# Copying u from PSUM instead of moving it by DMA, two output stores per block, and a new hand-written order

## The chip, the cores and the metric

The kernel runs on one core of a Trainium2 chip. The metric is the device time of one execution in microseconds (us), the median of several runs. The core has five engines that each work through their own instruction stream in order: PE (TensorE, matmuls), DVE (VectorE), ACT (ScalarE), POOL (GpSimd) and SP (SyncE, which here only issues DMA transfers). ACT issues some DMA transfers too.

## What is computed

The inputs r, k, v, w, a, b have the shape (4, 8, 768, 40): batch, heads, time steps, head width. For each of the 32 pairs of batch and head a 40x40 state is carried over the 768 steps:

```python
for t in range(S):
    y[:, :, t] = np.einsum('bhd,bhde->bhe', rt, state)
    Sa = np.einsum('bhde,bhe->bhd', state, at)
    state_decay = state * wt[:, :, None, :] - np.einsum('bhd,bhe->bhde', Sa, bt)
    state = state_decay + np.einsum('bhd,bhe->bhde', vt, kt)
```

The result, laid out as x of shape (4, 768, 320), goes through a gated convolution over time and two matrix products:

```python
h = np.maximum(x @ w_in, 0.0)            # w_in: 320 x 1024
conv_out = sum(conv_w[k] * hp[:, k:k + S, :] for k in range(3))   # hp is h, padded by one step on each side
gate = 1.0 / (1.0 + np.exp(-conv_out))
out = (h * gate) @ w_out                 # w_out: 1024 x 320
```

## The kernel before

**Tiling.** The 768 time steps are cut into 24 chunks of 32 (`C`, `NSTEP`); two chunks make a pair (index `j`, 12 of them) and also a window of 64 steps for the second part (`W`, 12 windows). Inside a chunk the recurrence is replaced by matrix products with a small triangular inverse.

**Per pair:** `load_wakb` brings in w, a, k, b; `decays` makes running products of w (`suf`, `pre`, two scans each on DVE); `decayed` makes the scaled a, k and b (`ah`, `kt`); `scores` multiplies them (`ps`) into `at`; `solve_in` writes a part of `at` through DRAM into `bb`; `solve` runs 31 dependent multiply-add pairs (`st`, `xx`, lines L566 and L572), for even pairs on DVE and for odd ones on POOL; the inverse `tt` comes back through DRAM.

**Per chunk n, the chain** (`chain`): `pp` = state times a, plus scores times v (PE, L598 and L608); `psb` = -pp (ACT, L615); `pu` = tt times psb (PE, L624), which is u in PSUM; then u goes into the tile `vu`. That tile has 128 partitions (four quadrants of 32) and a free index y of 0 or 1 in front of the heads; v has been loaded into two of the four quadrants for each y, and u fills the other two. After that `pn` = vu times kb (PE, L647), the new state = old state + pn (DVE, L659; in the first chunk a copy, L657) and its decay (POOL, L662), with which the next chunk starts. There are two `vu` tiles and two state tiles, used in turn.

**How u gets beside v before:** ACT copies all of `pu` into an SBUF tile `u` (L631), then ACT issues three transfers from `u` into `vu` (L635): quadrant 0 and quadrant 3 into y=1, and quadrants 1 and 2 together into y=0. `pn` and `pv` wait for all three.

**Outputs per chunk:** `vturn` turns vu (`pv`, L671, copied by ACT into `v`, L688); `pairs` makes `pm` and `ms`; `from_state` and `outputs` add up `py`; `finish` turns it (`pq`, L774), scales it (`xf`, DVE, L779) and splits it into `xh` (ACT) and `xl` (POOL).

**Per window:** `moe_in` makes four pieces `ph` (16 matmuls each, L814), the relu `hb`, the convolution `cc` (ACT L835, DVE L843), the sigmoid (ACT L848) and the gate product `g` (DVE L853); `moe_out` makes two blocks `po` (16 matmul instructions each, L861). A block covers two batches of 64 steps: 128 rows of 320 numbers. ACT copies it into the only buffer `ob` (L876) and SP stores it: in window 0 by two transfers of 63 rows (L882), in the other windows by one transfer whose DRAM side has the shape 2 x 64 x 320 (L886). At the end `moe_end` makes the last time step from `pe` (L861) through the same buffer, as `oe` (L907, L908).

**Weights** come as float64 words and are made into float32 by DVE, eight instructions a piece (L267 to L285), 23 pieces, all in the first third of the run.

**What sets the order.** Nothing is scheduled by a planner at run time: the table `ORDER` lists tokens such as `ch5` (the chain of chunk 5) or `mi3.2` (piece 2 of window 3), and each token lets that piece of work emit its instructions up to its next `yield`. So the table decides how the pieces are mixed in every engine's stream. A chain has nine such parts for n > 0; the fifth is the copy to `u`, the sixth the three transfers.

Of the kernel before, what the change touches and what calls it, by code (L numbers as in the profile page):

```python
# [17 lines left out]
C = 32  # L18
# [5 lines left out]
    tt=2, psb=1, u=1, sd=1, r64=1, vu64=1, ms=1, ysb=1, xf=1, xh=2, xl=2, xp=1, hb=2, cc=2, o=1,  # L24
# [9 lines left out]
we0 we1 ld0*2 we0 ld0 lv0*2 we1 we0 de0 we2 ld0*2 de0*2 dd0 we1 ld1 lv1*2 we2 we3 lr0*2 dd0*2 we2  # L34
we1*2 dd0*4 we2*2 ld1 dd0 we0*2 de1 ha0 de1*2 we4 ha0*2 fs0*2 dd0*2 we3 rt0 ha1 rt0*2 ha1*2 ld1 we3
dd1 we3*2 we4 we5 ld1*2 ld2 sc0 dd1*2 we4*3 we6 sc0*2 dd1 sc1 lr1*2 ch0 sc1*2 dd1 we5 dd1 we5 ch0
we5*2 dd1*2 de2 we7 de2*2 ha2 si0*2 ha2*2 we7 dd1*2 we6 we7*3 we8 so0 we6 ld2 we6*2 we9 ld2*3 so0
sc2*3 sc3*3 so0 dd2 si1*2 we9 so0 we9*3 we10 so0 ld3 so0*3 we8 so0*2 so1*2 we10 we8 dd2*2 we10*3
dd2*4 we11 we8*2 dd2 so1 we12 ch0 dd2*2 ch0*2 so1 ld3 we11 ld3 so1 sc4 we12 we11 we13 ch0*2 we12*3
sc4*2 vt0 we11*2 we14 sc5 lv2*2 vt0*2 ch0*2 sc5*2 ro0 pa0 so1 si2*2 pa0*2 ch1*2 we13*2 st1 ch1*2  # L40
st1*2 ou0 ch1 we14*2 ch1 so1 ha3*3 we15 we16 ou0*2 fs1*2 ro0*2 fi0*2 so1 fi0*3 vt1 we15*2 ch1 vt1*2
pa1 we17 pa1*2 so1*2 ch1 ou1 we16*2 ha4 ch1*2 ou1*2 fi1 ha4*2 rt1 ch2 rt1*2 fi1 ch2 we17*2 fi1 de3
ch2 fi1*2 st2*3 pk0*2 mi0.3*2 de3*2 we18 we19 ld3*2 ch2 so2 lv3*2 dd3 ch2*2 mi0.2*2 ld4 mi0.3
we19*2 mi0.2 fs2*2 mi0.3 mi0.2 we20 we18*2 mi0.3 lr2*2 mi0.2 vt2 we21 vt2*2 dd3*2 ch2 dd3*2 lv4*2
ch2 dd3*2 ch2*2 we20*2 pa2 we22 ld4 dd3 we21*2 st3 dd3*2 st3*2 ch3*2 pa2*2 we22*2 ch3 ou2 ld4 ch3
ou2*2 fi2 ch3 ha5 ch3 fi2 fs3*2 mi0.3 sc6 ha5*2 fi2 sc6*2 sc7 mi0.3 fi2*2 sc7*2 mi0.3*2 mi0.0 si3*2
mi0.1 mi0.2 mi0.1 vt3 ch3 so2 vt3*2 mi0.2 pa3 mi0.1 pa3*2 ch3 ou3 lv5*2 mi0.2*2 rt2 ch3*2 ou3*2
mi0.1*2 so2 fi3 lr3*2 mi0.0 rt2*2 st4*3 ch4*2 fi3 so2 fi3 mi0.0 fi3*2 pk1*2 de4 ha6 mi0.0 ch4 de4*2
dd4 ha6*2 mi0.0 ld4*2 ld5 so2 fs4*2 so2*3 mi0.1 so2*2 so3 dd4*2 mi0.1 so3 mi0.1*2 mi1.2 mi1.3 dd4*5
mi0.0 so3 dd4*2 mi0.0 mi1.3*2 ch4 mi0.0*2 mi1.0 ch4 so3 ch4 ld5 mi1.3*3 ld5 mi1.0*2 sc8 mi1.0*2  # L50
# [87 lines left out]
def tile_decay_delta_attention_then_conv_gate_moe(  # L138
# [45 lines left out]
    def quad(i):  # L184
        return slice(C * i, C * i + C)
# [829 lines left out]
```

## Time and profile before

| | before |
|---|---|
| median of 3 runs | 742.21 us (738.25 to 743.95) |
| the profiled execution, its own time | 741.73 us |
| its span, first to last instruction | 740.0 us |
| PE busy | 576.2 us (78%), 14265 matmuls |
| DVE busy | 439.7 us (59%), 1043 instructions |
| ACT busy (issuing transfers not counted) | 238.9 us (32%), 529 instructions |
| POOL busy | 228.9 us (31%), 466 instructions |
| mean granted TensorE clock | 0.835 of full speed |

Busy shares are averages over stages with different limits, so the profile is read by stage: when an engine is idle, the row of its next instruction says what ended last before it. The span is the part in which instructions ran; the execution's own time is 1.7 us longer.

### The profile page before, as it was taken

How to read it: one execution, taken by the hardware profiler on the slowest of the kernel's cores; microseconds unless marked ns; L12 is line 12 of the kernel's file. 1: busy time of each engine (PE TensorE's matmuls, PEld its weight loads, DVE VectorE, ACT ScalarE, POOL GpSimd, SP SyncE). 2: the span in 40 equal slices, each digit the busy share in tenths (PEclk: the TensorE clock that was granted, in tenths of full speed). 3: DMA queues.
4: the chain of work that ended last, by engine and by line, in shares of the span. 5: the costliest groups of instructions: out<-in, count | busy, mean ns of one | idle time of the engine just before them, and what ended most of it. 6: DMA issues, size and time to landing. Idle time of an engine off the chain costs nothing.

```text
span 740.0 us, 31943 instructions
## 1 busy us (share of the span) xinstructions
PE 576.2 (78%) x14265; PEld 490.5 (66%) x14265; DVE 439.7 (59%) x1043; ACT 238.9 (32%) x529; POOL 228.9 (31%) x466
## 2 busy tenths in 40 slices
PE   3634076678488788988988969889887998789995
PEld 2523065567377668777777858788687786768882
DVE  8878945966963764454874524965715695422550
ACT  1210012314232423434333135135333344344551
POOL 5101582001285101374002345014820017711100
PEclk9755557958868997997996899979977999899998
DMA  8999477673475356465563464644655425121000
GB/s 147 168 134 147 99 127 132 136 131 62 73 127 94 59 117 103 64 118 93 101 127 66 81 124 71 126 107 86 117 100 78 105 47 98 28 51 40 19 26 20
DMA packets 285345, 69.40 MB, mean 94 GB/s; under 512 B 258496, under 2 KB 281048, under 8 KB 285208
## 3 DMA queue, kind: packets, MB, share of 16 engines
q1 hardware_dynamic: 249280, 59.36, 44.6%
q10 hardware_dynamic: 35928, 7.99, 6.0%
q8 instruction: 112, 1.84, 1.1%
q14 instruction: 25, 0.20, 0.1%
HBM read 38.63 MB, written 10.22 MB: 66 GB/s over the span
## 4 chain that ended last, share of the span: by engine, by line
PE 47%; DVE 17%; DMA 14%; issue 7%; POOL 6%; SPq 3%; ACT 2%; ACTq 2%; DVEq 0%; POOLq 0%
PE po L861 9%; PE ph L814 9%; DMA vu<-u 4%; PE ps L510 3%; PE pm L715 3%; DVE xx L572 3%; PE pv L671 3%; PE pn L647 3%; DVE st L566 3%; PE py L753 2%; PE pu L624 2%; POOL st L566 2%; POOL xx L572 2%; PE pt L698 2%; PE pp L608 2%
## 5 line engine op out<-in xcount | busy, mean ns | idle before, releaser
L861 PE MATMUL po<-wo,g 128*128 128x320 f32 x384 | 117.6, 449 | 1.3 <-ACT hb L828 1.3
L843 DVE SCALAR_TENSOR_TENSOR cc<-hb,cw,cc 128x256 f32<-128x256 f32 x192 | 90.0, 532 | 44.1 <-ACT cc L835 44.1
L566 POOL TENSOR_TENSOR st<-xx,bb 128x126 f32<-128x126 f32 (+22 forms) x186 | 73.3, 394 | 67.5 <-DMA bb<-bd 31.3
L861 PEld LDWEIGHTS po<-wo,g 128*128 128x128 f32 x384 | 70.9, 196 | 26.1 <-issue 2.0
L662 POOL TENSOR_TENSOR state<-state,a 104x640 f32<-104x640 f32 x23 | 33.6, 1460 | 157.9 <-DVE state L659 139.2
L572 POOL TENSOR_TENSOR xx<-xx,st 128x126 f32<-128x126 f32 (+22 forms) x186 | 74.8, 402 | 14.6
L789 POOL TENSOR_TENSOR xl<-xf,xh 120x384 fp32r<-120x384 f32 x24 | 25.5, 1062 | 169.4 <-ACT xh L787 165.0
L814 PE MATMUL ph<-xh,wih 120*128 120x256 f32 x288 | 62.5, 330 | 0.8 <-ACT ob L876 0.8
L510 PE MATMUL ps<-a,k 40*64 40x32 f32 x1536 | 37.8, 249 | 29.0 <-issue 15.7
L828 ACT ACTIVATE hb<-ph 128x512 f32<-128x512 f32 x48 | 28.5, 598 | 91.0 <-PE ph L814 78.5
L510 PEld LDWEIGHTS ps<-a,k 40*64 40x64 f32 x1536 | 34.2, 168 | 34.1 <-issue 26.0
L572 DVE TENSOR_TENSOR xx<-xx,st 128x126 f32<-128x126 f32 (+22 forms) x186 | 52.7, 283 | 6.4
L566 DVE TENSOR_TENSOR st<-xx,bb 128x126 f32<-128x126 f32 (+22 forms) x186 | 50.7, 272 | 7.0 <-DMA bb<-bd 1.2
L814 PEld LDWEIGHTS ph<-xh,wih 120*128 120x128 f32 x288 | 46.8, 214 | 5.2 <-issue 1.6
L624 PE MATMUL pu<-psb,tt 32*32 32x40 f32 x1536 | 27.5, 230 | 26.8 <-DVE ah L460 17.5
L722 DVE TENSOR_TENSOR ms<-pm,tri 128x512 f32<-128x512 f32 x24 | 16.6, 690 | 48.7 <-PE pm L715 48.5
L853 DVE TENSOR_TENSOR g<-cc,hb 128x512 f32<-128x512 f32 x48 | 34.5, 728 | 18.3 <-ACT cc L848 9.1
L779 DVE TENSOR_TENSOR xf<-pq,pre 120x384 f32<-120x384 f32 x24 | 13.3, 554 | 52.6 <-PE pq L774 48.3
L624 PEld LDWEIGHTS pu<-psb,tt 32*32 32x32 f32 x1536 | 22.8, 132 | 32.1 <-issue 27.8
L835 ACT ACTIVATE cc<-hb,cw 128x256 f32<-128x256 f32 x96 | 42.6, 501 | 0.0
L814 PE MATMUL ph<-xl,wih 120*128 120x256 f32 x192 | 42.3, 304 | 0.1
L516 DVE TENSOR_TENSOR at<-ps,tris 128x512 f32<-128x512 f32 x24 | 16.6, 690 | 42.6 <-PE ps L510 42.6
(305 smaller groups left out, 1155.9 us busy)
## 6 DMA issues: line engine op xcount, KB each, us to landing
bb<-bd SPq DMA_DIRECT2D x24, 256.0 KB
w<-in_w_dram SPq DMA_DIRECT2D x24, 160.0 KB
a<-in_a_dram SPq DMA_DIRECT2D x24, 160.0 KB
k<-in_k_dram SPq DMA_DIRECT2D x24, 160.0 KB
vu<-in_v_dram SPq DMA_DIRECT2D x96, 40.0 KB
b<-in_b_dram SPq DMA_DIRECT2D x24, 160.0 KB
rin<-in_r_dram SPq DMA_DIRECT2D x24, 160.0 KB
k<-kt SPq DMA_DIRECT2D x24, 160.0 KB
```

The source lines that it names most:

```text
L510: nc.tensor.matmul(ps[half(z), x, y * 128 + hp * C : y * 128 + hp * C + C], k64[half(x, D), 2 * y + c, kp, z], a64[half(x, D), c, y, hp, z ...
L566: eng.tensor_tensor(t3, xx[:, 0:nj, i : i + 1].to_broadcast([128, nj, nt]), bb[:, i : i + 1, i + 1 :].to_broadcast([128, nj, nt]), ALU.mult,)
L572: eng.tensor_tensor(xx[:, 0:nj, i + 1 :], xx[:, 0:nj, i + 1 :], t3, ALU.add)
L624: nc.tensor.matmul(pu[bu(bi), 0, h * D : h * D + D], pd["tt"][quad(bi), c, 4 * x + hp], psb[quad(bi), x, hp], start=(h == 0), stop=True, s ...
L662: nc.gpsimd.tensor_tensor(new, new, al[..., 0:1].to_broadcast([SR, 2, 8, D]), ALU.mult)
L789: nc.gpsimd.tensor_tensor(wd["xl"][:, :, :, tw], xf, xh.bitcast(F32), ALU.subtract)
L814: nc.tensor.matmul(ph[:, j], l[:, fs], x, start=(j == 0 and i == 0), stop=(i == len(passes) - 1), skip_group_check=True,)
L828: nc.scalar.activation(out=hb[:, :, :, 2 : W + 2], in_=ph, func=AF.Relu)
L835: nc.scalar.activation(out=cc[:, j], in_=hb[:, j, :, 1 : W + 1], func=AF.Copy, scale=cw[:, 1, f : f + 1],)
L843: nc.vector.scalar_tensor_tensor(out=cc[:, j], in0=hb[:, j, :, x : W + x], scalar=cw[:, x, f : f + 1], in1=cc[:, j], op0=ALU.mult, op1=ALU ...
L853: nc.vector.tensor_tensor(g, cc, hb[:, :, :, 1 : W + 1], ALU.mult)
L861: nc.tensor.matmul(po[:rows, :DM], parts(f), wo[:, f, :], start=(f == 0), stop=(f == NF - 1))
```

## The change

Three things change.

1. The tile `u` and the three transfers go. Four copies read `pu` directly and write into `vu`, one for each quadrant of 32 partitions and 320 columns: ACT takes quadrants 1 and 2, DVE takes quadrants 0 and 3. Both reach their place without leaving their partitions, since only the free index y differs. The chain has one part less.
2. Every output block is stored by two transfers, one per batch (64 rows, in window 0 still 63), as it was before in window 0 alone.
3. The table `ORDER` is new throughout; of it the diff shows one line of each.

```diff
-    tt=2, psb=1, u=1, sd=1, r64=1, vu64=1, ms=1, ysb=1, xf=1, xh=2, xl=2, xp=1, hb=2, cc=2, o=1,
+    tt=2, psb=1, sd=1, r64=1, vu64=1, ms=1, ysb=1, xf=1, xh=2, xl=2, xp=1, hb=2, cc=2, o=1,
...
-pa1 we17 pa1*2 so1*2 ch1 ou1 we16*2 ha4 ch1*2 ou1*2 fi1 ha4*2 rt1 ch2 rt1*2 fi1 ch2 we17*2 fi1 de3
+vt1 we18 fs1*2 lv3*2 vt1*2 fi0*2 ch1 pa1 so1 rt1 pa1*2 ou1 lr2*2 rt1*2 ha3 ou1*2 ch1*2 fi1 ha3*2
...
-        uu = buf(wn, [128, H, D], "u", f"u{n}")
-        nc.scalar.copy(uu.rearrange("p h d -> p (h d)"), pu[:, 0, 0:HD])
-        yield
-
-        for rows, y in ((slice(0, C), 1), (slice(3 * C, 4 * C), 1), (slice(C, 3 * C), 0)):
-            nc.scalar.dma_start(vu[rows, y, :, 0:D], uu[rows])
+
+        for i, q in enumerate((1, 0, 2, 3)):
+            dst = vu[quad(q), int(q in (0, 3)), :, 0:D]
+            src = pu[quad(q), 0, 0:HD].rearrange("p (h d) -> p h d", d=D)
+            if i % 2:
+                nc.vector.tensor_copy(dst, src)
+            else:
+                nc.scalar.copy(dst, src)
         yield
...
-        if lo:
-            for x in range(BO):
-                nc.sync.dma_start(
-                    out[bo * BO + x, t0 - 1 + lo : t0 + W - 1, :], ob[x * W + lo : (x + 1) * W]
-                )
-        else:
-            nc.sync.dma_start(out[bs, t0 - 1 : t0 + W - 1, :], ob)
+        for x in range(BO):
+            nc.sync.dma_start(
+                out[bo * BO + x, t0 - 1 + lo : t0 + W - 1, :], ob[x * W + lo : (x + 1) * W]
+            )
```

What this moves in the streams is shown at three places. The first is ACT's stream around chunk 1's u, before:

```order
L615 ACTIVATE psb_1238<-pp_1156 128x320
L705 COPY sd_1273<-pt_1229 128x832
L631 COPY u_1307<-pu_1240 128x320
L635 DMA vu_119<-u_1307 32x8x40 x2
L635 DMA vu_119<-u_1307 64x8x40
L536 COPY kb_1339<-pz_1332 128x640
L760 COPY ysb_1349<-py_287 128x2x4x40
L787 CAST xh_1387<-xf_1393 120x12x32
```

and the same place of the changed kernel:

```order
L615 ACTIVATE psb_1243<-pp_1156 128x320
L762 COPY ysb_1310<-py_284 128x2x4x40
L637 COPY vu_119<-pu_1277 32x8x40 x2
L707 COPY sd_1343<-pt_1322 128x832
L789 CAST xh_1312<-xf_1345 120x12x32
```

The copy to u and three transfers have become two copies; `ysb` now stands ahead of them and `kb` elsewhere, so neither is behind a transfer.

The second place is PE's stream in the same chunk, from `pu` to the first reader of `vu_119`, before (`py` and `pq` are outputs, `pz` turns kt for a later chunk, `pv` turns vu):

```order
L624 MATMUL pu_1240<-psb_1238,tt_787 32x40 x32
L753 MATMUL py_287<-kb_285,ms_1154 32x40 x32
L529 MATMUL pz_1332<-ident,kt_471 128x120 x6
L739 MATMUL py_1351<-sd_1273,r_317 32x40 x32
L774 MATMUL pq_1389<-ident,ysb_1349 120x128 x3
L671 MATMUL pv_1406<-ident,vu_119 128x128 x8
```

and now (`pt` turns the state, `pn` is the state's update):

```order
L755 MATMUL py_284<-kb_282,ms_1233 32x40 x32
L624 MATMUL pu_1277<-psb_1243,tt_855 32x40 x32
L776 MATMUL pq_1314<-ident,ysb_1310 120x128 x3
L700 MATMUL pt_1322<-ident,state_125 128x104 x8
L649 MATMUL pn_1347<-vu_119,kb_303 64x40 x2
```

Four groups of other work between `pu` and the first reader have become two, and `pn` now stands ahead of `pv`.

The third place is DVE's stream with the copies of chunk 1, among a weight piece (`wo2`), the outputs (`xf`) and the next weight piece; before, DVE had no part in moving u:

```order
L282 SCALAR_TENSOR_TENSOR wo2q<-wo2s,wo2q 128x256
L285 TENSOR_TENSOR wo<-wo2q 128x256
L635 COPY vu_119<-pu_1277 32x8x40 x2
L781 TENSOR_TENSOR xf_1345<-pq_1314,pre_190 120x384
L267 TENSOR_SCALAR wo3q<-wo3r 128x256
```

DVE's two copies stand behind the eight instructions of a weight piece, of which the last two are shown.

## Rows read from the trace of the kernel before

**Rows 1.** Busy time by stage: length, then each engine's busy us (instructions)

```profile
core 0: us, PE busy (x) PEld busy (x) DVE busy (x) ACT busy (x) POOL busy (x), PEclk, DMA share, GB/s
0.00:100.00 100.00, 36.05 (x552) 30.74 (x552) 81.88 (x214) 10.68 (x25) 33.63 (x74) 0.65 0.88 140
100.00:220.00 120.00, 84.13 (x2387) 74.92 (x2388) 85.08 (x211) 34.83 (x69) 37.62 (x78) 0.76 0.60 111
220.00:720.00 500.00, 444.83 (x11300) 379.06 (x11293) 270.25 (x613) 191.52 (x432) 157.67 (x316) 0.89 0.44 83
```

**Rows 2.** Chain of work that ended last, 100 to 220 us: start, us, what

```profile
by line: DMA vu<-u 17.6%; PE pv L671 6.5%; DVE xx L572 6.4%; PE pn L647 5.6%; issue 5.5%; DVE st L566 5.3%; DMA bb<-bd 4.7%; DMA vu<-in_v_dram 3.6%; PE ps L510 3.3%; DMA tt<-xd 2.6%; DMA xd<-xx 2.4%; PE pu L624 2.4%; PE pm L715 2.3%; PE ph 
```

**Rows 3.** PE's waits, 100 to 220 us: total us, times, longest

```profile
PE pv L671 <- DMA vu<-u: 9.3, 3, 5.5
...
PE pq L774 <- ACT ysb L760: 3.2, 1, 3.2
```

**Rows 4.** PE's waits, 220 to 720 us

```profile
PE py L753 <- issue: 9.6, 7, 2.2
...
PE pv L671 <- DMA vu<-u: 2.2, 2, 1.9
```

**Rows 5.** ACT in order of time, chunk 1: start, us, what [idle before <-releaser]

```profile
112.97 0.42 ACT L631 COPY u<-pu 128x320 f32<-128x320 f32 x1 [0.40 <-PE pu L624]
113.43 3.93 ACTq L635 DMA_DIRECT2D vu<-u  x3
117.40 0.69 ACT L536 COPY kb<-pz 128x640 f32<-128x640 f32 x1 [4.00 <-DMA vu<-u]
117.99 0.43 ACT L760 COPY ysb<-py 128x320 f32<-128x320 f32 x1
```

**Rows 6.** Tile vu: issues of its transfers, ns min/median/max

```profile
L635 ACTq DMA_DIRECT2D vu<-u x72: 592/629/1964, 92.3 to 680.2; - x72
```

**Rows 7.** PE in order of time, the first reader of vu in chunks 1 and 2

```profile
121.90 1.97 PE L671 MATMUL pv<-ident,vu 128*128 128x128 f32 x8 [2.88 <-DMA vu<-u]
...
147.77 1.94 PE L671 MATMUL pv<-ident,vu 128*128 128x128 f32 x8 [5.45 <-DMA vu<-u]
```

**Rows 8.** DVE in order of time: first and last of four waits behind u

```profile
102.14 0.82 DVE L657 COPY state<-pn 104x640 f32<-104x640 f32 x1 [6.57 <-PE pn L647]
...
151.76 0.82 DVE L659 TENSOR_TENSOR state<-pn,state 104x640 f32<-104x640 f32 x1 [3.08 <-PE pn L647]
```

**Rows 9.** Groups of instructions near the new copies: count, busy us, mean ns

```profile
L779 DVE TENSOR_TENSOR xf<-pq,pre 120x384 f32<-120x384 f32 x24 | 13.3, 554 | 52.6 <-PE pq L774 48.3 <-POOL xx L572 4.4
...
L631 ACT COPY u<-pu 128x320 f32<-128x320 f32 x24 | 10.2, 426 | 42.3 <-PE pu L624 37.3 <-POOL st L566 4.9
...
L213 DVE TENSOR_SCALAR tris<-tri 32x128 f32<-32x128 f32 x8 | 2.8, 486 | 0.7 <-POOL tri L204 0.7
```

**Rows 10.** All engines in order of time, the end of the run

```profile
725.12 6.60 SPq L886 DMA_DIRECT2D out_dram<-ob  x2
726.72 4.47 PE L861 MATMUL pe<-wo,e 128*4 128x320 f32 x16
730.76 0.42 ACT L876 COPY ob<-po 128x320 f32<-128x320 f32 x1 [5.66 <-DMA out_dram<-ob]
736.83 0.41 ACT L907 COPY oe<-pe 4x320 f32<-4x320 f32 x1 [5.65 <-DMA out_dram<-ob]
```

**Rows 11.** DMA share and GB/s (last two) in stretches of output stores

```profile
239.80:240.90 1.10, 1.10 (x59) 1.05 (x38) 0.00 (x0) 1.07 (x4) 0.00 (x0) 1.00 0.45 149
726.20:730.40 4.20, 4.20 (x17) 1.30 (x16) 0.00 (x0) 0.00 (x0) 0.00 (x0) 1.00 0.13 39
```

**Rows 12.** SP issuing the two stores of window 0's first block

```profile
239.13 0.65 SPq L882 DMA_DIRECT2D out_dram<-ob  x2
```

**Rows 13.** DVE's longest runs that can stand ahead of a copy, 220 to 720 us

```profile
L843 DVE SCALAR_TENSOR_TENSOR cc<-hb,cw,cc 128x256 f32<-128x256 f32 x164 | 76.7, 532 | 39.5 <-ACT cc L835 39.5
...
L447 DVE TENSOR_TENSOR_SCAN pre<-pw,dp 120x396 f32<-120x396 f32 x14 | 13.0, 969 | 0.2
```

More of the change, by code (lines that the diff above doesn't have):

```diff
@@ L45 @@
[L45 to L50, printed above, removed]
@@ new lines @@
+so4 ch7 dd5*2 ch7 pa6 ch7 mi1.2*2 ch7 pa6*2 mi2.0 ch7 mi2.0 mo0.0*2 ou6 so4 ch7 ld6 ou6*2 fi6 st7
+ch7 mi2.0 fi6 ch7*2 so4 vt7 mi2.0 fi6 sc10 lv9*2 vt7*2 fi6*2 so4 mi2.0 ch8 st7*2 ch8 sc10*2 so4*2
+mi2.0 ch8 sc11 fs7*2 sc11*2 mi2.0 pa7 mi1.3 rt4 pa7*2 mi1.3 mi2.0*2 mi2.1 rt4*2 ou7 mi1.3*2 mi2.1
+lr5*2 st8 ou7*2 fi7 st8*2 mi2.1 fi7 si5*2 so5 de6 ch8 mi2.1 de6*2 fi7 mi2.1 dd6 ch8 mi2.3*3 mo1.1
+ld6*2 mi2.3*2 ha9 dd6*2 ld7 ch8 ha9*2 mi2.1 dd6*2 vt8 ld7 ch8 mo1.1 dd6 mo1.1 mi2.3 mo1.1 ha10
+vt8*2 dd6 ch8*2 mo1.0 ha10*2 dd6 fi7*2 mi2.1 mo1.1*2 ch9 mi2.3 mi2.1*2 so5 ch9 mi2.3*2 fs8*2 ch9
@@ new lines @@
+dd8 so7 ch12 mo3.0 ld9 dd8*2 mi4.2 mo3.0 ha13*2 ld9 mi4.3 mo3.0 dd8 ch12*2 mi4.3*2 vt12 dd8*2 so7
+ch13 vt12*2 ch13 mi4.0*2 ch13 mo3.0*2 ch13 mi4.0 so7 lv14*2 ha14 fs12*2 ha14*2 mi4.0 ch13 pa12
+mi4.0 ch13 pa12*2 so7 mi4.0 pk5*2 ou12 vt13 ou12*2 ch13 sc16 vt13*2 ch13*2 fi12 sc16*2 lv15*2 sc17
+fi12 so7 fi12 ch14 sc17*2 ch14 si8*2 st13 fi12*2 ch14 ha15 st13*2 mo3.1 ha15*2 mi4.2 mo3.1 mi4.0
+mi4.2*2 mo3.1 mi4.0*2 so7*2 so8 mo3.1 mi5.0*3 mi5.1 mi5.0 mi5.1*2 fs13*2 pa13 mi5.1 mi5.0*2 mi5.1
+st14 mo4.0 st14*2 pa13*2 mi5.0 rt7 mo3.1*2 mi5.1 ou13 rt7*2 lr8*2 mi5.0*2 ch14 ou13*2 mi5.1 so8
@@ new lines @@
+fi13 mi5.2 ch14 mi5.2*2 ha16 fi13 ch14 ha16*2 mi5.1*2 fi13 so8 de9 mi5.2*2 fi13*2 vt14 ld9*2
+mi5.3*2 vt14*2 lv16*2 ch14 mi5.3 de9*2 ch14*2 dd9 pk6*2 fs14*2 mi5.3*2 mo4.0*2 ld10 mo4.0 dd9 mi5.3
+pa14 dd9 mo4.0*2 dd9*2 pa14*2 mo4.1 ld10 dd9*2 mi5.2 ch15 ld10 ou14 dd9 mi5.2 ch15 ou14*2 mi5.2*2
+dd9*2 ch15 fi14 st15 fi14 so8 fi14 ch15 st15*2 fi14*2 mi6.0*2 ch15 mi6.0 ha17 so8 ch15 ha17*2
+mi6.0*2 vt15 mo4.1 mi5.3 lv17*2 vt15*2 ch15 mi6.0 mo4.1 ch15*2 mo4.1 mi5.3*2 so8 sc18 mi6.0 mo4.1*2
+ch16*2 sc18*2 sc19 ch16 so8 mi6.1*3 sc19*2 fs15*2 so8 si9*2 pa15 mi6.1*2 mi6.0*2 st16 pa15*2
@@ new lines @@
+sc23*2 ha21 lv21*2 vt19*2 so10 mo6.1 ha21*2 mo6.1 si11*2 fs19*2 mi7.2*2 pa19 mi7.3*2 so10 st20
+mi8.0*2 st20*2 mi8.0 mo6.1*2 so10 rt10 mi8.0 mi8.1*2 mi8.0 lr11*2 so10 rt10*2 mi8.1 mo7.1 mi8.0
+so10*2 so11 mi8.1*2 mo7.1 mi8.1 mi8.0 mo7.1*2 mi8.0*2 pa19*2 mi8.3 so11 mi8.1 mi8.3*2 mi8.1*2 ou19
+mi8.3 mi8.2 ou19*2 mi8.2 mi8.3 so11 fi19 mi8.3 mi8.2 mo7.1*2 ha22 fi19 fs20*2 ha22*2 fi19 ch20
+mi8.2*2 mo7.0 fi19*2 pk9*2 mi8.2 ch20 mo7.0 so11 mi8.3 mi8.2 mo7.0 mi8.3*2 ch20 mi8.2*2 mo7.0 ch20
+so11 vt20 mo7.0*2 mi9.2*2 vt20*2 mi9.2 lv22*2 pa20 ch20*2 mi9.2*2 mi9.3 pa20*2 mi9.3 mi9.2 so11
@@ new lines @@
+ou20 ch21 ou20*2 fi20 mi9.2 st21 fi20 mi9.2*2 fi20 ch21 st21*2 mi9.3 fi20*2 mi9.1 so11 mi9.3 ch21
+mi9.0 mi9.1 mi9.3*2 mi9.1 ch21 so11 mi9.1 fs21*2 mi9.3 ch21 ha23 mi9.3*2 mi9.1 ch21 so11*2 mi9.1
+ha23*2 mo8.1 mi9.0 ch21 mi9.0 ch21*2 vt21 mi9.0 mo8.1 vt21*2 st22 mi9.0*2 pa21 st22*2 lv23*2 ch22
+pa21*2 ch22 rt11 ch22*2 rt11*2 ou21 ch22 mo8.1 ou21*2 fi21 ch22 fi21*2 vt22 ch22 fi21*2 pk10*2
+mo8.1 ch22*2 fs22*2 vt22*2 mo8.1*2 ch23*2 pa22 ch23*2 pa22*2 ch23*2 ou22*3 vt23 fi22 vt23*2 st23
+fi22 mo8.0 fi22 mi9.1 fi22*2 mi9.0 mo8.0 mi9.1*2 st23*2 mi10.3*2 mi9.0*2 mi10.3 mo8.0 mi10.3*2
@@ new lines @@
+mo8.0 mi10.3 mi10.1*2 mo8.0*2 mi10.1 fs23*2 pa23 mi10.1 mi10.3 mi10.1 mi10.3*2 mi10.2 pa23*2
+mi10.2*2 mi10.1 ou23 mi10.2 mo9.0 ou23*2 mi10.1 mi10.2 fi23 mi10.1*2 mi10.0 fi23 mi10.0 mi10.2
+mi10.0 mo9.0 fi23 mo9.0 mi10.0*2 fi23*2 pk11*2 mi10.0 mo9.0 mo9.1 mi10.2 mo9.0*2 mi10.0 mo9.1
+mi10.2*2 mi11.1*2 mi10.0*2 mi11.1 mo9.1 mi11.1*2 mi11.0 mi11.1 mi11.0*2 mo9.1 mo10.0 mi11.0 mi11.1
+mo9.1*2 mo10.0 mi11.0 mi11.1*2 mi11.0 mi11.3*3 mo10.0 mi11.3 mi11.0 mo10.0 mi11.0*2 mi11.2*2 mi11.3
+mo10.0*2 mi11.2 mi11.3 mo10.1 mi11.2 mi11.3 en0 mo10.1 mi11.2 mi11.3*2 mo10.1 mi11.2 mo10.1 mi11.2
@@ L118 @@
+mo10.1*2 mi11.2*2 mo11.1*4 mo11.0 mo11.1*2 mo11.0*5 en0*2
 """
```

123 lines of the change are left out of this document (46 added, 77 removed).

## Prediction

> **What bounds the kernel now.** I read the busy times by stage first. In the first 100 us PE is busy for 36 us and DVE for 82 [rows 1]: the weights are being unpacked on DVE and the first inverse is solved there, and PE mostly waits. From 100 to 220 us PE is busy for 84 of 120 us and DVE for 85: neither is full, so something that is no engine's work stands in the chain. From 220 to 720 us PE is busy for 445 of 500 us: 55 us are left to win there in all. The last 20 us are a tail of their own.
>
> The chain of work between 100 and 220 us, followed back from its last instruction, says what stands in it: 17.6% of 120 us, 21.1 us, is the transfer of u into `vu`, its largest share [rows 2]. PE's waits agree: for that transfer `pv` waited 9.3 us in three places [rows 3], of which the chunks 1 and 2 have 2.88 and 5.45 us [rows 7]. After 220 us the same wait is 2.2 us in two places, less than a quarter of one `py` wait with no visible cause (9.6 us) [rows 4]. So the transfer is a cost of the early stage. Later, matmuls of other chunks and of the second part lie between `pu` and the readers and cover it.
>
> In chunk 1 the reader sees how it works. ACT copies u at 112.97 us, is busy issuing the three transfers until 117.36, and only then makes `kb` and `ysb` [rows 5]; `pq` waits 3.2 us for that `ysb` [rows 3]; the transfers have landed when `pv` starts at 121.90 [rows 7], 8.5 us after the copy to u ended at 113.39.
>
> The end of the run is the third place. The only `ob` buffer must be stored before the next block may be copied into it. The copy of the last block waits 5.66 us for the store of the one before, and the copy of `oe` waits 5.65 us for the store of the last block; `pe`, which `oe` also needs, is ready at 726.72 + 4.47 = 731.19 us, long before 736.83 [rows 10].
>
> **Part 1: u without transfers.** For each chunk a copy of 0.43 us on ACT [rows 9] and three issues with a median of 0.63 us [rows 6] go: 0.43 + 1.89 = 2.3 us of ACT, then the landing. Four copies of 32 partitions x 320 columns come. Such a copy is in no row. On ACT the nearest row is the old copy, 320 columns in 426 ns [rows 9]; I take 0.43 each, 0.86 for two. On DVE 640 columns from PSUM take 0.82 us [rows 8] and 384 take 0.554 [rows 9], about 1.05 ns a column, so 320 give 0.554 - 64 x 0.00105 = 0.49 us, 0.97 for two. The upper bound is the only DVE row on 32 partitions, 128 columns in a mean of 486 ns while POOL worked beside it [rows 9]; with 192 more columns that is 0.69, or 1.38 for two. The lower bound is ACT's 0.43. I take 0.49, because its rows too read PSUM. So u is in place about 1.0 us after `pu` where it took 8.9 in chunk 1 (112.97 to 121.90).
>
> What PE gains from 100 to 220 us: the 9.3 us of `pv` waits and the 3.2 us of `pq` behind ACT's issuing, 12.5 us in all. In each of these waits the copies would have ended well before PE ran out of other work (chunk 1: PE became idle at 121.90 - 2.88 = 119.0, the copies would end near 114). What DVE pays there: five chunks x 0.97 = 4.9 us. DVE is idle for 120 - 85 = 35 us of this stage, and 18.3 us of it are four waits that themselves stand behind u, of which the first is 6.57 and the last 3.08 us [rows 8]; they cover the copies and shrink with them. I take 12 us. The bounds are 21.1 us (all that the chain shows) and -4.9 us (DVE turns out to be the stage's limit, the waits move to its weight pieces, and the copies come on top).
>
> After 220 us: 2.2 us of `pv` waits, and some of ACT's lateness; I take 3 us, bounds 0 and 6. The DVE copies, 19 chunks x 0.97 = 18 us, lie in 230 us of DVE idle time (500 - 270) [rows 1].
>
> **Part 2: the store in two transfers.** The single store runs at 39 GB/s with a DMA share of 0.13, which is two of sixteen engines, for 4.2 us; window 0's two transfers ran at 149 GB/s and a share of 0.45, and were through in 1.1 us [rows 11]. Issuing two took SP 0.65 us [rows 12], so a second costs 0.33. A store gets shorter by 4.2 - 1.1 - 0.33 = 2.8 us. In the tail two stand in series: 725.12 + 5.64 - 2.8 = 727.96 for the copy of the last block, again 0.45 + 2.85 us, and `oe` can be copied at 731.3, just after `pe` at 731.19, in place of 736.83. That is 5.5 us. Elsewhere stores are hidden. SP gets 22 issues more, 7 us over the run, which I cost at nothing: the loads they stand among are issued a chunk or more ahead.
>
> The Trainium skill ("DMA: Bandwidth & Descriptors", section "Rules for kernel authors") says of two transfers to disjoint partition halves "Don't bother", since both halves use the same 16 engines and serialize. By it this term would be 0 and the sum 5.5 us less. The same table says that an outermost dimension of c < 16 confines a transfer to c engines; the old store's DRAM side is 2 x 64 x 320, and the share of 0.13 agrees with that second rule.
>
> **Part 3: the order.** ORDER decides how much other work lies between `pu` and its reader. In chunk 1 four groups have become two, a short `pq` and `pt`; they and the copies take about the same time (1 to 2 us). The rest of the redraw I cannot price from a row: all engines do the same work, so it can only move waits. I take 0. As bounds I take 11 us either way, half of the 36 - 12.5 = 23 us of PE idle time from 100 to 220 us that have other causes.
>
> **Sum:** 12 + 3 + 5.5 + 0 = 20.5 us off the profiled execution's 741.7 us, 721.2; that execution was 0.5 us under the median of the runs, so 722.
>
> **The rivals.**
> - *The order closes other gaps too* (chance 0.20): PE's idle time before 220 us has causes beyond u, such as runs of the solve on DVE that now are mixed with other work. 722 - 11 = 711, and less with all 21.1 us of the chain. Against it: DVE has the same work.
> - *DVE is the early limit* (0.16): DVE is 82% busy in the first 100 us and 71% in the next 120 [rows 1], and chunk 1's copies now stand behind a weight piece of eight instructions. Then the 12 us don't come and 4.9 are added: 742.2 - 3 - 5.5 + 4.9 = 738.6, within 1%. Against it: the 18.3 us of DVE waits behind u.
> - *Slower: the copies wait in DVE's stream* (0.07). Before, the chain did not touch DVE between `pu` and `pn`. A convolution run of four takes 4 x 0.53 = 2.1 us, two scans 1.9 [rows 13]; a copy that arrives behind one makes `pn`, the state and the next chunk late, with only 1 to 2 us of cover. It takes all the gain at 20.5 / 24 = 0.85 us per chunk; at 1.5 us in every chunk the time is 722 + 36 = 758. Against it: DVE idles for 46% of the long stage.
> - *The halves serialize* (0.05): the two stores follow one another on the same engines and take 4.2 us together. 727.5.
>
> **How the numbers follow.** The forecast as summed has a chance of 0.52, with its own range of 713 to 730 (the early term between 5 and 21). Changes of about 1% are what a measurement of this kernel can tell from none. Faster by over 1% (under 734.8): 0.52 + 0.20 + 0.05 = 0.77. Within 1%: 0.16. Slower: 0.07. The range is 703 (11 us from the order and 8 more of the chain) to 739 (DVE as the early limit); outside are the slow rival, the far part of the first one, and what goes wrong in two places.
>
> **What the profile after would show.** No `DMA vu<-u` in any wait or chain; the first reader of `vu` in chunks 1 and 2 without a wait of 3 to 5 us; DVE and ACT copies of 0.4 to 0.5 us each; PE busy for more of the stretch from 100 to 220 us, or chunk 5 reached some 12 us earlier; waits of `ob` and `oe` at the end of under 3 us. I am wrong if the new copies take 0.7 us or more, if `pn` or `pv` wait for DVE by 1 us in most chunks, if DVE's share in the early stage rises to 90% with the same pace, or if the tail after `pe` is still 8 us long.

## The result and the profile after

The kernel after takes 722.86 us, the median of 4 runs (721.62 to 724.23); the kernel before, beside it, took 742.18 us. The ratio is 0.9747 with a 95% interval of 0.9704 to 0.9791, so it is 19 us faster, between 15.5 and 22. Timed once more beside other kernels it had 0.9721 (0.9663 to 0.9778). The forecast was 722 us. The total is right; of the four terms that make it, only the store's is. Ratios and intervals, here and below, leave out executions that were more than 1.5% above their kernel's fastest, so a ratio is not always that of the two medians given.

| | before | after |
|---|---|---|
| the profiled execution, its own time | 741.73 us | 721.62 us |
| its span | 740.0 us | 719.9 us |
| PE busy | 576.2 us (78%) | 579.1 us (80%) |
| DVE busy, instructions | 439.7 us, 1043 | 466.2 us, 1091 |
| ACT busy, instructions | 238.9 us, 529 | 251.9 us, 553 |

PE does the same work; it waits less. The lines of the kernel after are numbered two higher than before from the copies on, up to the store. The three stages of [rows 1], with the columns of that group:

```profile
core 0: us, PE busy (x) PEld busy (x) DVE busy (x) ACT busy (x) POOL busy (x), PEclk, DMA share, GB/s
0.00:100.00 100.00, 39.05 (x620) 34.01 (x621) 82.95 (x219) 12.30 (x28) 28.06 (x62) 0.73 0.91 149
100.00:220.00 120.00, 92.16 (x2674) 81.78 (x2672) 98.03 (x226) 39.28 (x80) 52.14 (x108) 0.77 0.53 105
220.00:700.00 480.00, 430.84 (x10912) 372.68 (x10912) 281.20 (x637) 195.97 (x435) 149.65 (x296) 0.88 0.43 78
```

From 100 to 220 us PE is busy for 8 us more than before, and so is DVE for 13. PE's longest waits in that stage, total us, times and the longest; the largest one before, which [rows 3] leaves out, stands first (`issue`: the profile shows nothing that was waited for):

```profile
PE pb L429 <- DVE ah L460: 10.1, 1, 10.1
```

```profile
PE ph L816 <- DMA xp<-xh: 8.4, 2, 5.6
PE pp L608 <- issue: 4.5, 2, 2.5
PE pv L673 <- DVE state L661: 2.4, 1, 2.4
```

No wait for a transfer of u is left; it was the largest that the change was aimed at [rows 3], and the second largest of the stage. The wait of `pb` for `ah` is gone too. The wait for the transfer of `xh` into `xp` has grown, from 2.1 us in two places to 8.4. All engines in order of time in chunk 1, the copies of u and the first reader of `vu`:

```profile
112.10 0.76 PE L624 MATMUL pu<-psb,tt 32*32 32x40 f32 x32 [0.40 <-issue]
...
112.92 0.42 ACT L637 COPY vu<-pu 32x320 f32<-32x320 f32 x1 [1.40 <-PE pu L624]
...
113.37 0.48 DVE L635 COPY vu<-pu 32x320 f32<-32x320 f32 x1 [0.24 <-ACT vu L637]
...
113.88 0.42 ACT L637 COPY vu<-pu 32x320 f32<-32x320 f32 x1 [0.54 <-DVE vu L635]
...
114.33 0.50 DVE L635 COPY vu<-pu 32x320 f32<-32x320 f32 x1 [0.48 <-ACT vu L637]
...
115.00 1.93 PE L649 MATMUL pn<-vu,kb 64*64 64x40 f32 x64
```

`pu` ends at 112.86, u is complete at 114.83, and `pn` begins at 115.00. Before, the reader came at 121.90 [rows 7]. The copies do not run side by side, as the forecast had it: each waits for the one before, ACT, DVE, ACT, DVE, so that four copies of 0.42 to 0.50 us take 1.9 us (112.92 to 114.83) and not 1.0.

The end of the run, to be read beside [rows 10]:

```profile
704.49 9.78 SPq L883 DMA_DIRECT2D out_dram<-ob  x6
...
708.39 0.42 ACT L878 COPY ob<-po 128x320 f32<-128x320 f32 x1 [3.40 <-PE po L863]
712.54 4.47 PE L863 MATMUL pe<-wo,e 128*4 128x320 f32 x16
712.69 0.42 ACT L878 COPY ob<-po 128x320 f32<-128x320 f32 x1 [3.88 <-PE po L863]
717.09 0.41 ACT L906 COPY oe<-pe 4x320 f32<-4x320 f32 x1 [3.98 <-PE pe L863]
```

ACT still waits here, 3.4 to 4.0 us where it was 5.7, but for PE and no longer for a store: `oe` is copied at 717.09, and `pe` ended at 712.54 + 4.47 = 717.01. The stores themselves, in stretches of one block each, with the DMA share and GB/s last as in [rows 11]:

```profile
705.60:706.70 1.10, 1.10 (x6) 0.78 (x5) 0.12 (x1) 0.00 (x0) 0.00 (x0) 1.00 0.63 148
709.90:711.10 1.20, 1.20 (x6) 0.81 (x5) 0.00 (x0) 0.00 (x0) 0.00 (x0) 1.00 0.58 137
```

A block is through in 1.1 us at 140 GB/s where it took 4.2 at 39.

**Where the time went.** To compare kernels whose orders differ, I cut the span at two points that all have: the end of `pu` of chunk 4 and of chunk 23. Up to the first, PE has run the same 2794 matmuls in each of these kernels. The three stretches, before and then after:

```profile
0.00:210.90 210.90, 112.04 (x2794) 98.62 (x2794) 161.50 (x415) 41.21 (x83) 63.48 (x134) 0.71 0.72 124
210.90:678.30 467.40, 411.35 (x10900) 351.47 (x10899) 256.70 (x580) 173.19 (x384) 163.43 (x331) 0.87 0.48 89
678.30:740.00 61.70, 52.80 (x581) 40.38 (x574) 21.47 (x48) 24.52 (x63) 2.00 (x2) 0.95 0.09 24
```

```profile
0.00:197.70 197.70, 114.07 (x2794) 101.57 (x2794) 167.17 (x422) 42.47 (x88) 64.11 (x137) 0.74 0.70 126
197.70:658.10 460.40, 406.34 (x10942) 351.16 (x10942) 275.49 (x618) 182.36 (x399) 163.73 (x328) 0.87 0.47 85
658.10:719.90 61.80, 58.66 (x536) 45.59 (x534) 23.55 (x51) 27.06 (x67) 2.00 (x2) 0.95 0.09 23
```

The early stretch is 13.2 us shorter, 210.9 to 197.7. The other two belong together, because the new order has moved work across the second cut: behind it PE now has 45 matmuls fewer, but 16 long ones of `po` more, and is busy 58.66 - 52.80 = 5.9 us longer. Together they went from 529.1 us to 522.2, 6.9 us less. Three changes were made at once, so these differences are not yet anybody's. The experiments divide them.

### The profile page after: what moved, and what is told of

Same layout as the page of the kernel before. It is cut to its first block, busy times and chain, and to the rows that moved or that the text cites. A ratio compares the mean times of both kernels' runs of the same rounds, so it can differ in the third digit from the quotient of the medians.

```text
span 719.9 us, 31917 instructions
## 1 busy us (share of the span) xinstructions
PE 579.1 (80%) x14265; PEld 498.3 (69%) x14265; DVE 466.2 (65%) x1091; ACT 251.9 (35%) x553; POOL 229.8 (32%) x466
## 4 chain that ended last, share of the span: by engine, by line
PE 26%; issue 6%; DMA 5%; DVE 5%; POOL 4%; ACT 2%; SPq 2%; ACTq 1%; POOLq 0%; DVEq 0%
PE po L863 7%; PE ph L816 5%; DMA bb<-bd 2%; PE pm L717 2%; POOL xx L572 2%; POOL st L566 2%; PE pv L673 1%; DMA bd<-at 1%; PE ps L510 1%; PE pn L649 1%; PE pp L608 1%; PE pt L700 1%; PE py L755 1%; PE pp L598 1%; PE pu L624 1%
## 5 line engine op out<-in xcount | busy, mean ns | idle before, releaser
L863 PE MATMUL po<-wo,g 128*128 128x320 f32 x384 | 120.5, 460 | 5.4 <-ACT hb L830 3.5
L863 PEld LDWEIGHTS po<-wo,g 128*128 128x128 f32 x384 | 73.5, 201 | 31.8 <-issue 5.6
L572 POOL TENSOR_TENSOR xx<-xx,st 128x126 f32<-128x126 f32 (+22 forms) x186 | 77.6, 417 | 14.6
L566 DVE TENSOR_TENSOR st<-xx,bb 128x126 f32<-128x126 f32 (+22 forms) x186 | 55.8, 300 | 13.8 <-DMA bb<-bd 8.2
L635 DVE COPY vu<-pu 32x320 f32<-32x320 f32 x48 | 23.3, 486 | 46.9 <-ACT vu L637 46.9
L510 PE MATMUL ps<-a,k 40*64 40x32 f32 x1536 | 36.0, 246 | 10.5 <-issue 5.3
L510 PEld LDWEIGHTS ps<-a,k 40*64 40x64 f32 x1536 | 32.7, 165 | 15.1 <-issue 9.0
L717 PE MATMUL pm<-r,v 40*64 40x32 f32 x1536 | 34.0, 240 | 6.0 <-issue 4.9
L608 PE MATMUL pp<-vu,at 32*32 32x40 f32 x1536 | 25.9, 222 | 15.4 <-issue 15.4
```

The lines of the kernel that those rows point to most:

```text
L510: nc.tensor.matmul(ps[half(z), x, y * 128 + hp * C : y * 128 + hp * C + C], k64[half(x, D), 2 * y + c, kp, z], a64[half(x, D), c, y, hp, z ...
L566: eng.tensor_tensor(t3, xx[:, 0:nj, i : i + 1].to_broadcast([128, nj, nt]), bb[:, i : i + 1, i + 1 :].to_broadcast([128, nj, nt]), ALU.mult,)
L572: eng.tensor_tensor(xx[:, 0:nj, i + 1 :], xx[:, 0:nj, i + 1 :], t3, ALU.add)
L608: nc.tensor.matmul(pp[quad(bi), x, hp * D : hp * D + D], at[kv(bi), c, y, x, hp], vu[kv(bi), y, KEY[x][hp], 0:D], start=(first and hp == 0 ...
L717: nc.tensor.matmul(pm[half(z), x, y * 128 + i * C : y * 128 + i * C + C], v64[half(x, D), y, i, half(z)], r64[half(x, D), y, i, quad(2 * z ...
L863: nc.tensor.matmul(po[:rows, :DM], parts(f), wo[:, f, :], start=(f == 0), stop=(f == NF - 1))
```

## The experiments

Each kernel was timed five more times beside its profiled run and beside runs of the kernel before, whose medians were 744.6 us (first four kernels), 743.4 (next four) and 744.7 (last four). "Stretches" are the three above, cut in each kernel's own profile.

**The split store alone.** Old order, transfers of u as before:

```diff
-        if lo:
-            for x in range(BO):
-                nc.sync.dma_start(
-                    out[bo * BO + x, t0 - 1 + lo : t0 + W - 1, :], ob[x * W + lo : (x + 1) * W]
-                )
-        else:
-            nc.sync.dma_start(out[bs, t0 - 1 : t0 + W - 1, :], ob)
+        for x in range(BO):
+            nc.sync.dma_start(
+                out[bo * BO + x, t0 - 1 + lo : t0 + W - 1, :], ob[x * W + lo : (x + 1) * W]
+            )
```

> The kernel before, with the store of every block in two transfers and nothing else: transfers of u and old order stay. Theory (tail term 5.5 us): a store lands in about 1.1 us in place of 4.0, the copy of the last block and that of oe each wait some 2.8 us less, and the time is 742.2 - 5.5 = 736.7. Rival, the halves serialize on the same engines: both halves together still take about 4 us and the time stays at 742.2.

Measured: 735.1 us, ratio 0.9887 (0.9848 to 0.9927), 8.4 us less with an interval of 5.4 to 11.3. In its profile the first two stretches are those of before within 0.7 us (210.3 and 466.7), and the last is 56.1 us in place of 61.7:

```profile
677.00:733.10 56.10, 52.84 (x575) 40.41 (x574) 21.41 (x48) 24.48 (x63) 2.00 (x2) 0.99 0.11 25
```

So the tail gives 5.6 us, as costed, with the same PE work in it. The rival, that both halves still take about 4 us, is refuted. The 2.8 us between 5.6 and 8.4 are no more than the interval.

**The copies alone, old order.** The chain's sixth part stays as an empty step:

```diff
...
-        uu = buf(wn, [128, H, D], "u", f"u{n}")
-        nc.scalar.copy(uu.rearrange("p h d -> p (h d)"), pu[:, 0, 0:HD])
-        yield
-
-        for rows, y in ((slice(0, C), 1), (slice(3 * C, 4 * C), 1), (slice(C, 3 * C), 0)):
-            nc.scalar.dma_start(vu[rows, y, :, 0:D], uu[rows])
+        for i, q in enumerate((1, 0, 2, 3)):
+            dst = vu[quad(q), int(q in (0, 3)), :, 0:D]
+            src = pu[quad(q), 0, 0:HD].rearrange("p (h d) -> p h d", d=D)
+            if i % 2:
+                nc.vector.tensor_copy(dst, src)
+            else:
+                nc.scalar.copy(dst, src)
+        yield
         yield
```

> The kernel before, with the four copies in place of the copy to u and its three transfers, single store and old order kept (the chain's sixth part is left empty, so that every other instruction keeps its place). Theory (early term 12, late term 3): 742.2 - 15 = 727. Rival, the gain needs the new order: with the old order less than 5 us is gained, 737 or more. Rival, copies wait in DVE's stream, where the old order left no room for them: pn waits for DVE's copies by 1 us or more in most chunks and the time is over 742.

Measured: 733.4 us, ratio 0.9865 (0.9820 to 0.9909), 10.0 us less (6.8 to 13.4). The 15 us of the forecast lie outside. Its stretches are 201.7, 468.3 and 61.4: in the profile all of the gain is before chunk 5, and nothing comes from the long stretch. The rival of over 742 us is refuted by the time.

**Both, old order**, timed twice:

> The copies and the split store under the old order; to the kernel after it lacks only the new order. Theory (order worth 0): 742.2 - 20.5 = 721.7, the same as the kernel after (722.9) within its interval. Rival, the order closes gaps of its own or makes room for the copies: 728 to 734, and the difference to 722.9 is the order's share. Rival, the new order costs: under 718.

Measured: 728.6 us, ratio 0.9785 (0.9734 to 0.9835), in the range of the first rival. The stretches:

```profile
0.00:205.00 205.00, 113.37 (x2794) 99.93 (x2794) 166.48 (x423) 42.84 (x87) 62.80 (x134) 0.74 0.70 124
205.00:672.10 467.10, 408.89 (x10900) 348.31 (x10899) 276.33 (x618) 181.25 (x403) 163.28 (x331) 0.88 0.45 83
672.10:728.00 55.90, 52.68 (x576) 40.42 (x574) 22.44 (x50) 24.97 (x64) 2.00 (x2) 0.99 0.09 22
```

What was lost of the early term shows in PE's waits from 100 to 220 us of the kernel with the copies alone:

```profile
PE pb L429 <- DVE ah L460: 9.8, 1, 9.8
PE ph L816 <- DMA xp<-xh: 3.3, 2, 1.8
...
PE pn L649 <- ACT v L690: 2.2, 1, 2.2
PE pp L608 <- issue: 1.8, 1, 1.8
```

The waits for the transfers of u are gone and that for `ysb` is down from 3.2 to 0.2 us. But PE now waits up to 2.4 us at a time for other things or with no visible cause (`py`, `pn`, `pp`) and 1.0 us for a copy of u, and one wait of 10 us near 200 us is as long as it was. In the kernel with both parts its rows on PE and DVE are these (start, us, instruction):

```profile
186.97 0.87 PE L429 MATMUL pk<-ident,k 128*120 128x128 f32 x6 [0.20 <-DVE pre L447]
197.96 1.51 PE L429 MATMUL pb<-ident,b 128*120 128x128 f32 x6 [10.12 <-issue]
```

```profile
182.84 1.85 DVE L438 TENSOR_TENSOR_SCAN suf<-pw,dsuf 120x396 f32<-120x396 f32 x2
...
185.06 1.85 DVE L447 TENSOR_TENSOR_SCAN pre<-pw,dp 120x396 f32<-120x396 f32 x2
186.83 0.27 DVE L566 TENSOR_TENSOR st<-xx,bb 128x135 f32<-128x135 f32 x1
...
195.17 0.19 DVE L572 TENSOR_TENSOR xx<-xx,st 128x16 f32<-128x16 f32 x1
195.27 1.66 DVE L845 SCALAR_TENSOR_TENSOR cc<-hb,cw,cc 128x256 f32<-128x256 f32 x4
196.85 1.01 DVE L460 TENSOR_TENSOR ah<-pa,pre 120x384 f32<-120x384 f32 x2
```

The transposes `pb` wait for `ah` on DVE (the waits of the kernel with the copies alone name it). The old order puts `ah` behind the last 30 instructions of a solve, from 186.83 to 195.36, and behind a convolution run. (The 44 of an expectation below are these and the 14 ahead of the scans.) DVE works through it without a gap and waits for no u in it, so copying u faster cannot shorten it: both engines only get there sooner. In the new order the same work stands the other way round, the end of the solve first, then the scans and `ah` at once, and this `pb` has no wait (last row):

```profile
187.24 0.19 DVE L572 TENSOR_TENSOR xx<-xx,st 128x16 f32<-128x16 f32 x1
187.34 1.84 DVE L438 TENSOR_TENSOR_SCAN suf<-pw,dsuf 120x396 f32<-120x396 f32 x2
...
189.56 1.85 DVE L447 TENSOR_TENSOR_SCAN pre<-pw,dp 120x396 f32<-120x396 f32 x2
191.33 1.00 DVE L460 TENSOR_TENSOR ah<-pa,pre 120x384 f32<-120x384 f32 x2
192.86 1.49 PE L429 MATMUL pb<-ident,b 128*120 128x128 f32 x6
```

The solve in these rows also decides when the early stretch ends. In the kernel before, the chain into chunk 4's `pu` runs from the solve's last instruction over the inverse's way through DRAM (start, us, what), and the kernel with the copies alone has the same chain:

```profile
201.21 0.19 DVE xx L572
202.10 2.90 DMA xd<-xx
206.52 3.10 DMA tt<-xd
209.66 1.28 PE pu L624 x58
```

In every profile of this document the solve ends 9 to 12 us before the early stretch does: at 201.4 us before, at 191.9, 195.4 and 195.2 in the three kernels with alternating copies under the old order, at 187.4 in the kernel after. So the stretch got shorter as DVE got to the end of this solve sooner, and PE's 10 us in front of `pb` stand beside that chain, not in it.

**The order's share**, the same two kernels side by side on one chip:

> The kernel after once more, on the chip and beside the runs of before that the next three share. Nothing is changed; all expect the ratio 0.975 of its first timing within the interval. The next kernel lacks only its order.

> Copies and split store under the old order, timed beside the kernel after itself, so that their difference is the order's share. Theory formed from the traces so far (the old order leaves PE a 10 us wait near 200 us for a run of 44 solve instructions on DVE, which the new order does not have; some of it is given back by waits of 1 to 3 us in the new order): 4 to 8 us above the kernel after. Rival, the order is worth nothing as the prediction took it: within 2 us of it.

Measured: the kernel after 718.5 us, ratio 0.9721 (0.9663 to 0.9778); under the old order 728.9 us, 0.9851 (0.9801 to 0.9901). The intervals do not meet: the new order is worth 5.7 us (728.6 against 722.9, timed apart) to 10.4 us (here, more than the 8 that I allowed). The second profile under the old order has an early stretch of 204.7 us, and the kernel after 197.5 in its own: 7.2 us. That the solve's earlier end brings this is read from the rows; no run moved it alone. The two later stretches together are 522.2 and 518.6 us here, but 523.0 and 522.2 in the other pair, so what the order does after chunk 5, 1 to 4 us, is not settled.

**The old transfers under the new order**, copy and transfers in the chain's one part:

```diff
-        for i, q in enumerate((1, 0, 2, 3)):
...
+        uu = buf(wn, [128, H, D], "u", f"u{n}")
+        nc.scalar.copy(uu.rearrange("p h d -> p (h d)"), pu[:, 0, 0:HD])
+        for rows, y in ((slice(0, C), 1), (slice(3 * C, 4 * C), 1), (slice(C, 3 * C), 0)):
+            nc.scalar.dma_start(vu[rows, y, :, 0:D], uu[rows])
```

> The kernel after with the copy to u and its three transfers put back in place of the four copies (both in the one part of the chain); split store and new order stay. Theory: the new order leaves only 1 to 2 us of work between pu and its first reader, so about 8.5 us of transfer stand open in the early chunks; PE's waits for u come to more than the 9.3 + 2.2 us of before and the time is above 742 - 5.5 = 737, about 745 if ten chunks wait 1 us more each. Rival, the order itself is what made the kernel faster: 728 or less.

Measured: 797.5 us, ratio 1.0729 (1.0680 to 1.0779), much more than I expected. Tile `vu`, what ended PE's idle time before its readers and who waited for it:

```profile
  DMA vu<-u: 65.3, 20
...
  PE pn L646: 57.2, 18
```

```profile
122.86 1.93 PE L646 MATMUL pn<-vu,kb 64*64 64x40 f32 x64 [5.88 <-DMA vu<-u]
```

Readers of `vu` wait for the transfer in 20 places, 65.3 us in all, where before PE had five such waits of `pv`, 9.3 + 2.2 us [rows 3, 4], and one of `pn`, 0.8 us. Chunk 1 alone (second fence, PE in order of time) has 5.88 us. My ten chunks by 1 us more were a guess. The new order has taken the cover away in the late chunks too: the long stretch is 522.7 us, against 460.4 in the kernel after. So the order gains only together with the copies: alone it would be 797.5 - 722.9 = 75 us worse than with them.

**One store per block under the new order:**

> The kernel after with one transfer per block again (windows 1 to 11), copies and new order kept: the tail term alone, under the new order. Theory (a long store delays the next copy into the only ob buffer by 2.8 us, and twice in series at the end): 5.5 us above the kernel after, and the copy of oe waits for the store and not for pe. From the split alone under the old order 8.4 us (2.9 more than the tail's two waits explain) could come here too. Rival, the halves share the same engines and the split gains nothing: within 2 us of the kernel after.

Measured: 730.6 us, ratio 0.9809 (0.9756 to 0.9863). Its last stretch is 66.0 us long against the 61.8 of the kernel after, 4.2 us for the split; `oe` waits for the store again:

```profile
717.70 0.43 ACT L878 COPY ob<-po 128x320 f32<-128x320 f32 x1 [5.67 <-DMA out_dram<-ob]
723.77 0.41 ACT L909 COPY oe<-pe 4x320 f32<-4x320 f32 x1 [5.65 <-DMA out_dram<-ob]
```

By the ratios the split is worth 4.6 to 6.6 us here, with intervals that overlap those of the kernel after.

**Which engine copies.** The sequence ACT, ACT, DVE, DVE; all four on ACT (twice); all four on DVE:

```diff
-        for i, q in enumerate((1, 0, 2, 3)):
+        for i, q in enumerate((1, 2, 0, 3)):
...
-            if i % 2:
+            if i > 1:
```

```diff
-            if i % 2:
-                nc.vector.tensor_copy(dst, src)
-            else:
-                nc.scalar.copy(dst, src)
+            nc.scalar.copy(dst, src)
```

For four on DVE the line that stays is `nc.vector.tensor_copy(dst, src)`.

> The kernel after with the same four copies in another sequence: ACT's two (quadrants 1 and 2) first, then DVE's two, in place of ACT, DVE, ACT, DVE. One engine change is left of three. Theory, the handing over between the engines costs: u is complete some 0.2 us sooner where both are free, DVE waits once instead of twice in a chunk, 24 x 0.1 to 0.3 us and so 2 to 6 us less in all if PE waits for it everywhere; 0 to 3 us less expected, since PE mostly has other work. Rival, DVE's wait gets longer because ACT's two copies stand before its first: no change or up to 3 us more.

> The kernel after with all four copies on ACT: 4 x 0.42 = 1.7 us in one piece where the alternation took 1.9, nothing on DVE, 24 x 2 x 0.49 = 23 us of DVE's time free, ACT 20 us more. Theory, DVE is a limit before 220 us (98 of 120 us busy) and its copies queue behind its other work: 2 to 6 us faster than the kernel after. Rival, the copies cost DVE nothing that matters: within 2 us. Rival, ACT's copies now stand behind ACT's relu and sigmoid and its issuing: 2 to 5 us slower.

> The kernel after with all four copies on DVE: 4 x 0.49 = 1.95 us in one piece, 24 x 2 x 0.49 = 23 us more of DVE's time, 20 us less of ACT's. Theory, DVE's spare time after 220 us covers it and before 220 us five chunks cost 5 x 0.97 = 5 us at most: 0 to 5 us slower than the kernel after. Rival, the copies stand behind other work on DVE and everything behind them is late: 1 us in every chunk, 24 us slower. Rival, which engine copies does not matter: within 2 us.

> The kernel after with all four copies on ACT, once more, beside the two others of this set. Theory, DVE's 23 us count only where DVE is the limit, before 220 us: 2 to 5 us under the kernel after and 3 to 8 under the one with four copies on DVE. Rival, neither matters: the same as the kernel after.

| kernel | median us | ratio to before | 95% interval | early stretch us |
|---|---|---|---|---|
| after (two timings) | 722.9, 718.5 | 0.9747, 0.9721 | 0.9663 to 0.9791 | 197.7, 197.5 |
| ACT, ACT, DVE, DVE | 717.2 | 0.9673 | 0.9612 to 0.9735 | 197.5 |
| four on ACT (two timings) | 716.1, 715.0 | 0.9672, 0.9594 | 0.9544 to 0.9732 | 197.1, 197.7 |
| four on DVE | 723.8 | 0.9729 | 0.9677 to 0.9782 | 201.3 |

Four on DVE and four on ACT, timed side by side, do not overlap (0.9677 to 0.9782 against 0.9544 to 0.9644): it matters where the copies run, by 8.8 us of the medians. (The first timing of four on ACT, beside other kernels, does overlap with four on DVE.) The early stretch shows 4 us of it, 201.3 against 197.1 and 197.7: with four on DVE the solve ends at 190.8 us in place of 187.4. Taking the two copies off DVE gains nothing there. The rest isn't in PE's waits: in the profiles the kernel with four on ACT has no less PE idle time than the kernel after (714.9 - 567.5 = 147.4 us against 719.9 - 579.1 = 140.8), only less PE busy time, and the second profile of the kernel after, with 716.1 us, is just 1.2 us longer. That four on ACT beat the kernel after is likely (both ratios lie below both of after), but only the second timing's interval lies clear of them, and I have no wait that explains it. I also expected DVE's 46.9 us of waiting for ACT's copies to cost something:

```profile
L635 DVE COPY vu<-pu 32x320 f32<-32x320 f32 x48 | 23.3, 486 | 46.9 <-ACT vu L637 46.9
```

With one handing-over left instead of three the ratio is lower by 0.005, within its interval. Not settled.

**Four on ACT under the old order:**

> Copies and split store under the old order, with all four copies on ACT. Under that order PE waits 10 us near 200 us until DVE has worked through a run of 44 solve instructions, the convolution and the scaling of a. Theory, DVE is late there, and its two copies in each of five chunks before make it later: without them that stretch comes up to 4.9 us sooner and the time is 2 to 5 us under the 728.8 of the same kernel with alternating copies. Rival, the wait comes from the order of DVE's stream alone and moves with whatever released it: within 2 us of 728.8.

Measured: 721.5 us (711.8 to 730.1), ratio 0.9631 (0.9568 to 0.9694). The profile (of the run of 730.1 us) says the rival is right on the mechanism: the early stretch is 205.4 us and the wait of `pb` for `ah` is 10.1 us, both as with alternating copies, although DVE had its copies taken away; the solve ends at 196.4 us. The 10 us stand in the order of DVE's stream, not in its load. The time, though, fell by some 7 us, more than the rival and the theory allowed, as it did under the new order with four copies on ACT, and that remains unexplained in the same way.

## Why the prediction was right, and where its steps were not

**What bounds the kernel: right.** The transfers of u stood in the early chain, and without them PE's waits for them are gone from every view. Two readings were wrong beside it: the list of PE's waits behind [rows 3] has the 10.1 us of `pb` above the 9.3 us that I took, and the 9.6 us of `py` were seven waits of at most 2.2 us, not one.

**The early term, 12 us: too large for the copies.** Each wait that I added up did go, and I took its whole length as gain because the copies would be done in time. That is the step that failed: I did not ask of each wait what was late next. What was late next is DVE's solve: PE's waits for u ended, but chunk 4's `pu` still had to wait for the inverse, whose solve ended 6 to 10 us sooner and not 12. Under the old order the early stretch shrank from 210.9 and 210.3 us (the two profiles with transfers) to 201.7, 205.0 and 204.7 (the three with alternating copies), 6.8 us in the mean; the three differ by 3.3 us though they do the same up to there, so this is good to some 3 us. On PE the rest shows as waits of 1 to 2.4 us of `py`, `pn` and `pp`, and the 10 us wait for DVE's `ah` stayed. I had seen the 23 us of "other causes" and left them in the bounds of the order only; the 10 us wait was the largest single one among them.

**The late term, 3 us: about 0.** From chunk 5 to chunk 23 the old order took 467.4 and 466.7 us with transfers, and 468.3, 467.1 and 465.4 with copies. The late waits for u were small and were replaced.

**The store, 5.5 us: right.** 5.6 us under the old order (61.7 to 56.1) and 4.2 under the new (66.0 to 61.8). `oe` follows `pe` by 0.08 us, as forecast. I had said that the waits of `ob` and `oe` would be under 3 us; they are 3.4 to 4.0, because PE, not the store, now ends last. The Trainium skill's "Don't bother" ("DMA: Bandwidth & Descriptors", section "Rules for kernel authors") does not hold for this transfer: the split took it from 4.2 us to 1.1. The second rule of the same section, on the outermost dimension, agrees with the single store's share of 0.13, two engines of sixteen, and sets no such bound for the halves with their 64 rows, which ran at about 0.6. No run kept one transfer with another outermost dimension, so that it is the dimension and not the number of transfers is not shown by itself.

**The order, 0: too small.** It is worth 5.7 to 10.4 us by the timings. In the early stretch it is 6.2 us (203.8, the mean of the three, to 197.6), and by the rows the mechanism is that of the first rival: the solve on DVE stands among other work in a new way and ends 8 us sooner. The copies on DVE are not what held it under the old order: with all four on ACT that stretch is as long, 205.4 us. It makes up for most of what the early and the late term lack (6.8 + 0 + 5.6 + 6.2 = 18.6 us, against 12 + 3 + 5.5 + 0 = 20.5; measured 19), so the total came out right by errors of opposite sign, which is luck. The reason that I gave, "it can only move waits", was no reason for 0: a moved wait that meets other work is a gain.

**The other rivals.** That DVE is the early limit has some truth: its solve ends the stretch, and four copies on DVE cost 4 us there. But the alternating copies did not take the gain back. That copies wait in DVE's stream and make `pn` late did not happen: after 220 us `pn` waited for DVE's copies by 1.8 us in two places.

**The copies' own cost: right in the parts, wrong in the sum.** 486 ns on DVE (estimate 0.49) and 416 on ACT (0.43), but one after another, so that u is in place 2.0 us after `pu` and not 1.0. In chunk 1 that cost PE next to nothing: `pq` and `pt` fill the 2.1 us from 112.86 to 115.00.

## What to carry to other kernels

When a wait is removed, look for what the waiting engine meets next, and take as gain only the part up to there; the largest wait that has another cause will still stand. Ask also which chain ends the stage: here it ran over DVE's solve and DRAM, and PE's longest wait was not in it. Price a new order by the largest gaps that it could close, each from a row, instead of by 0; and expect an order drawn for one hand-over to be very bad with another. Look at the DRAM side of a store: with an outermost dimension of 2 it ran at a share of 0.13 of the DMA engines, and two transfers were nearly four times as fast as one.

## What the runs showed of the hardware that I had not expected

- A copy of 32 partitions by 320 columns costs as much as one of 128 partitions: 416 ns on ACT, where the copy of all four quadrants to `u` took 426 [rows 9]. Four quadrants moved apart cost four copies.
- The four copies read four different quadrants of the same PSUM tile, and still each waited for the one on the other engine (46.9 us of DVE's waiting in 41 places in the kernel after). The Trainium skill ("PSUM — Partial Sum Buffer", section "PSUM bank collisions raise a hardware error") says that two engines may access different quadrants of one bank at the same time. No run here shows them doing so: in chunk 1, above, each copy starts only after the one before has ended. The four also write into one tile, `vu`, and which of the two shared tiles the waits are for is not shown.
